# The second mixture of a fused attention kernel in blocks of 512 tokens in place of 256

## The chip, the cores and the metric

The kernel runs on one core of a Trainium2 chip. The metric is the time of one execution on the device in microseconds (us); the median of several executions stands for a kernel. A core has TensorE (PE; its weight loads stand in the profile as PEld), VectorE (DVE), ScalarE (ACT), GpSimd (POOL), and SyncE (SP), whose queue issues the transfers (DMA) here. TensorE writes its results to PSUM, in banks of 512 floats on each of 128 partitions; everything else lies in SBUF.

## What is computed

Causal attention with a bias from cumulated sums, then two dense mixtures one after the other, over 4 x 576 = 2304 tokens of 512 features, each with a hidden layer of 2048. All of it is in float32. The second mixture, which is the one changed, is the last function:

```python
# attention: batch, n_heads, seq, head_dim = (4, 8, 576, 64) -> x: 2304 x 512
def _moe_ref(x, w_in, w_out):              # first mixture
    h = x @ w_in                           # 2304 x 2048
    g = h * (1.0 / (1.0 + np.exp(-1.702 * h)))
    return g @ w_out                       # 2304 x 512

def _moe2_ref(x, w_in, w_out, s, b):       # second mixture
    h = x @ w_in
    r = np.maximum(h, 0.0)
    g = s * (r * r) + b
    return g @ w_out
```

## The kernel before

**Split operands.** A float32 operand of a matmul is split into two parts of the type fp32r: a copy rounded to that type, and the remainder (the value less its copy). A product takes three matmuls: weight remainder by token copy, copy by remainder, copy by copy. A split token or weight tile therefore has two halves, `[:, 0]` the copy and `[:, 1]` the remainder.

**Tiling.** The hidden layer is cut into 16 slices f of 128, the features into four chunks of 128. For a slice f, `h2` issues 4 x 3 = 12 matmuls with a 128 x 128 piece of the weights as the stationary operand and the tokens, as many as the block has, as the moving one. They add up in one PSUM bank `ph`. Then a chain of five instructions makes the gated values: Relu (ACT) into `r`, square and scale-and-shift (both DVE, in place), the rounded copy (ACT), the remainder (POOL for even f, DVE for odd f) into `g`. On the way out, for each 128 tokens t, three matmuls with a 128 x 128 piece of g as stationary operand and 512 columns of the output weights as the moving one add into a bank `py[t]`, over all f. When f = 15 is in, `py[t]` is copied to SBUF (ACT or DVE) and stored.

**Order.** TensorE's instructions stand in the order of the program text; a planner puts those of the other engines into each engine's queue, and they wait there for semaphores. `second` runs over a block of 256 tokens: hidden matmuls of f, then the out-matmuls of f - 4 (`LEAD = 4`). So from f = 4 to 15 twelve hidden matmuls of 256 columns alternate with six out-matmuls of 512 columns; at the end of a block five groups of out-matmuls (30) stand together, and behind them five groups of hidden matmuls (60) of the next block. There are nine blocks.

**Tokens and weights.** The first mixture leaves its result in DRAM (`x1_d`, feature by token). `load_x` brings a block of it back in one transfer of 512 KB and splits it with two ACT copies and two POOL subtractions of 512 columns each. The last unit of the first mixture, `first_whole`, frees the first mixture's weights slice by slice; `next_weights` then brings the second mixture's: 32 weights (w2i and w2o, 16 each) of 512 KB come as 8-byte words into 5 staging places (tag `pair`), and `load_w` turns each into floats and splits it with two ACT and three DVE instructions (L128 to L136). A staging place is free again when its weight is split. All of this is issued on SP's one queue.

**Buffers.** `ph` takes 3 banks, `py` 5. `g` has 10 places of 640 floats, one for the two halves of a slice; `r` has 2 places of 320 floats (tag `th`, which the first mixture uses as well). `xT` in the pool `xp` has 4 places of 640 floats, used by the first mixture's tokens.

Of the kernel before, what the change touches and what calls it, by code (L numbers as in the profile page):

```python
# [9 lines left out]
F32 = mybir.dt.float32  # L10
U32 = mybir.dt.uint32
F32R = mybir.dt.float32r
AF = mybir.ActivationFunctionType
ALU = mybir.AluOpType
# [3 lines left out]
P = 128  # L18
# [11 lines left out]
SPAN = 0.98  # L30
EARLY = 1.0
AHEAD, LEAD = 2, 4


def f32(ap):
    return ap.bitcast(F32)
# [27 lines left out]
def fused_kernel(ctx: ExitStack, tc: tile.TileContext, qkT, vP, s, w1i, w1o, w2i, w2o, s2, b2, out):  # L64
    nc = tc.nc
    B, H, _, _ = qkT.shape
    D, S = P // 2, s.shape[1]
    BH = B * H
    NT, C = out.shape
    NF, _, CM = w1i.shape  # L70
    NC = C // P
# [4 lines left out]

    first, second = [(0, 64), (64, 192), (192, 320)], [(320, 448), (448, 576)]
    units = [Unit(b, 0, first, []) for b in range(B)] + [Unit(b, 1, second, first) for b in range(B)]
    NMAX = max(u.n for u in units)

# [32 lines left out]
    def load_w(stage, src, tag, f):  # L113

        pool, stage_tag, bufs = stage
        if src.dtype == F32:
            single = pool.tile([P, 2 * CM], F32, tag=stage_tag, name="single", bufs=bufs)[:, :CM]
            nc.sync.dma_start(single, src[f])
        else:

            pair = pool.tile([P, 2 * CM], U32, tag=stage_tag, name="pair", bufs=bufs)
            nc.sync.dma_start(pair, src[f].bitcast(U32))
            lower, upper = pair[:, 0 : 2 * CM : 2], pair[:, 1 : 2 * CM : 2]
            nc.scalar.activation(f32(upper), f32(upper), AF.Prelu, scale=2.0**-112, alpha=2.0**32)  # L128
            nc.vector.tensor_scalar(out=lower, in0=lower, scalar1=2.0**-29, scalar2=7.49, op0=ALU.mult, op1=ALU.min)  # L129
            nc.vector.scalar_tensor_tensor(  # L130
                out=lower, in0=upper, scalar=3, in1=lower, op0=ALU.logical_shift_left, op1=ALU.bitwise_or
            )
            single = f32(lower)
        w = wp.tile([P, 2, CM], F32R, tag=tag, name=f"{tag}{f}")
        nc.scalar.activation(w[:, 0, :], single, AF.Copy)
        nc.vector.tensor_tensor(w[:, 1, :], single, f32(w[:, 0, :]), ALU.subtract)  # L136
        return w


    with ExitStack() as p1:  # L140
# [4 lines left out]
            out=mask[:, WIDE:], in_=mask[:, WIDE:], pattern=[[-1, P]], compare_op=ALU.is_ge,  # L145
# [330 lines left out]
                run(ui)  # L476


    N2 = 256
    rawp = ctx.enter_context(tc.tile_pool(name="rawp", bufs=5))  # L480
    psY = ctx.enter_context(tc.tile_pool(name="psY", bufs=5, space=PSUM))
    xp2 = ctx.enter_context(tc.tile_pool(name="xp2", bufs=2))
    wi2, wo2 = {}, {}

    def load_x(ti):
        raw = xp2.tile([P, NC, N2], F32, tag="xraw2", name="xraw2", bufs=1)
        nc.sync.dma_start(raw, x1_d[:, ti * N2 : (ti + 1) * N2].rearrange("(c p) t -> p c t", p=P))
        x = xp2.tile([P, 2, NC, N2], F32R, tag="xT2", name="xT2")
        for cc in range(0, NC, 2):
            nc.scalar.activation(x[:, 0, cc : cc + 2, :], raw[:, cc : cc + 2, :], AF.Copy)  # L490
            nc.gpsimd.tensor_tensor(x[:, 1, cc : cc + 2, :], raw[:, cc : cc + 2, :], f32(x[:, 0, cc : cc + 2, :]), ALU.subtract)
        return x

    def h2(f, x, g2):
        ph = psM.tile([P, 512], F32, tag="m", name="ph2")
        k = 0
        for cc in range(NC):
            wc = slice(cc * P, (cc + 1) * P)
            for a, b in ((1, 0), (0, 1), (0, 0)):
                nc.tensor.matmul(ph[:, :N2], wi2[f][:, a, wc], x[:, b, cc, :], start=(k == 0), stop=(k == 3 * NC - 1))  # L500
                k += 1
        r = gp.tile([P, NMAX], F32, tag="th", name="r", bufs=2)[:, :N2]
        nc.scalar.activation(r, ph[:, :N2], AF.Relu)  # L503
        nc.vector.tensor_tensor(r, r, r, ALU.mult)  # L504
        nc.vector.tensor_scalar(out=r, in0=r, scalar1=s_sb, scalar2=b_sb, op0=ALU.mult, op1=ALU.add)  # L505
        g = gp.tile([P, 2, NMAX], F32R, tag="g", name="g2")
        nc.scalar.activation(g[:, 0, :N2], r, AF.Copy)  # L507
        (nc.vector if f % 2 else nc.gpsimd).tensor_tensor(g[:, 1, :N2], r, f32(g[:, 0, :N2]), ALU.subtract)  # L508
        g2[f] = g

    def first_whole(ui):

        n, x = units[ui].n, split_x(ui)
        py = [psY.tile([P, 512], F32, tag="y", name="py3") for _ in range(NC)]
        for f in range(NF + LEAD):
            if f < NF:
                yield from h_item(ui, f, x)
                freed.append(("wi", f))
            if f >= LEAD:
                k = f - LEAD  # L520
                for c in range(NC):
                    for i, (a, b) in enumerate(((1, 0), (0, 1), (0, 0))):
                        nc.tensor.matmul(
                            py[c][:, :n], wo[k][:, a, c * P : (c + 1) * P], g_t[ui, k][:, b, :n],
                            start=(k == 0 and i == 0), stop=(k == NF - 1 and i == 2),
                        )
                freed.append(("wo", k))
                yield 12 * (n / 2.4 + 3)
        for c in range(NC):
            y = gp.tile([P, NMAX], F32, tag="y", name="y", bufs=4)  # L530
            if c % 2:
                nc.scalar.activation(y[:, :n], py[c][:, :n], AF.Copy, scale=0.5)
            else:
                nc.vector.tensor_scalar(out=y[:, :n], in0=py[c][:, :n], scalar1=0.5, scalar2=None, op0=ALU.mult)
            nc.sync.dma_start(x1_d[c * P : (c + 1) * P, t0_of[ui] : t0_of[ui] + n], y[:, :n])

    def second(ti, x):
        g2 = {}
        py = [psY.tile([P, C], F32, tag="y", name="py2") for _ in range(N2 // P)]
        for f in range(NF + LEAD):  # L540
            if f < NF:
                h2(f, x, g2)
                yield 12 * (N2 / 2.4 + 3)
            if f >= LEAD:
                k = f - LEAD
                for t in range(N2 // P):
                    for i, (a, b) in enumerate(((1, 0), (0, 1), (0, 0))):
                        nc.tensor.matmul(  # L548
                            py[t], g2[k][:, a, t * P : (t + 1) * P], wo2[k][:, b, :],
                            start=(k == 0 and i == 0), stop=(k == NF - 1 and i == 2),  # L550
                        )
                yield 6 * 216
        for t in range(N2 // P):
            y = xp2.tile([P, C], F32, tag="y2", name="y2", bufs=3)
            if t % 2:
                nc.scalar.activation(y, py[t], AF.Copy)
            else:
                nc.vector.tensor_copy(y, py[t])
            r0 = ti * N2 + t * P
            nc.sync.dma_start(out[r0 : r0 + P, :], y)  # L560

    freed = []
    with tc.manual_schedule(engines={PE}):
        def next_weights():
            for tag, f in freed:
                src, to = (w2i, wi2) if tag == "wi" else (w2o, wo2)
                to[f] = load_w((rawp, "pair", 5), src, tag, f)
            freed.clear()

        x2 = load_x(0)  # L570
        for _ in first_whole(len(units) - 1):
            next_weights()
        next_weights()
        for ti in range(NT // N2):
            x = x2
            for k, _ in enumerate(second(ti, x)):
                if k == NF // 2 and ti + 1 < NT // N2:
                    x2 = load_x(ti + 1)


# [41 lines left out]
```

## Time and profile before

| | us |
|---|---|
| Median of 3 executions (1089.58 to 1094.0) | 1090.66 |
| The profiled execution | 1089.36 |
| Its span, from the first to the last instruction | 1087.6 |
| TensorE busy in the span | 1031.3 |
| VectorE busy | 681.9 |
| ScalarE busy | 556.8 |
| GpSimd busy | 349.5 |
| Mean granted clock of TensorE, as a share of 2.4 GHz | 0.983 |

The profile shows one execution. Durations of TensorE's matmuls overlap, since they are pipelined and their ends are modelled; what one of them costs in a run is the distance from its start to the next one's start. A line such as L500 is a line of the kernel before. `A <- B` reads as output from inputs, by the program's names, and `x12` counts instructions. In a row of the order of time, the first number is the start and the second the time from the first start to the last end of the merged instructions; in brackets stands how long the engine was idle before and what it waited for.

### The profile page before, as it was taken

The page shows a single profiled execution, that of the slowest core. Times are in us where ns is not written, and L with a number is a line of the kernel's source. Part 1 is how long each engine was busy: PE and PEld are TensorE (multiplying, and loading weights), DVE is VectorE, ACT ScalarE, POOL GpSimd, SP SyncE. Part 2 cuts the span into 40 slices and gives each one's busy share as a digit, 9 for nine tenths or more (in the row PEclk, how much of TensorE's full clock was granted, in tenths as well). Part 3 has the DMA queues.
Part 4 walks back from the last instruction along what each step waited for, and adds up shares of the span by engine and source line. Part 5 has one row for each costly group of instructions (what it writes and reads, how often), then busy time and mean ns, then how long its engine had stood idle before and what let it go on. Part 6 is the DMA issues. An engine that isn't in the chain of part 4 may idle for free.

```text
span 1087.6 us, 19218 instructions
## 1 busy us (share of the span) xinstructions
PE 1031.3 (95%) x6984; PEld 952.9 (88%) x6984; DVE 681.9 (63%) x1600; ACT 556.8 (51%) x1378; POOL 349.5 (32%) x412
## 2 busy tenths in 40 slices
PE   4978999999989999999999998899999999999998
PEld 2447999999988999999999998799989999899997
DVE  4689777566467788877886598843434434344333
ACT  4788766556536646656666476532323323233232
POOL 1124445335344435544453341121221212112110
PEclk9968999999999999999999998899999999999999
DMA  6566332121042232223221478210110101100000
GB/s 197 155 240 202 101 88 68 54 87 43 10 130 70 69 99 73 84 73 90 74 85 37 168 227 245 78 40 1 40 36 4 40 1 39 39 1 20 2 20 20
DMA packets 40799, 85.64 MB, mean 79 GB/s; under 512 B 5344, under 2 KB 20064, under 8 KB 40704
## 3 DMA queue, kind: packets, MB, share of 16 engines
q1 hardware_dynamic: 40704, 84.41, 25.2%
q8 instruction: 55, 0.90, 0.4%
q14 instruction: 40, 0.33, 0.1%
HBM read 70.30 MB, written 10.03 MB: 74 GB/s over the span
## 4 chain that ended last, share of the span: by engine, by line
PE 73%; DVE 13%; DMA 7%; ACT 4%; issue 3%; SPq 1%; POOL 0%; DVEq 0%; ACTq 0%; POOLq 0%
PE py L548 18%; PE ph L500 18%; PE py L404 13%; PE ph L382 12%; PE ps L249 4%; PE pst L287 4%; PE po L314 3%; DVE hi L111 3%; DMA pair<-w1i 2%; DMA pair<-w2i 2%; DVE pair L130 2%; DMA pair<-w1o 1%; DVE pair L129 1%; DVE x L255 1%; ACT x L261 1%
## 5 line engine op out<-in xcount | busy, mean ns | idle before, releaser
L382 PE MATMUL ph<-xT,wi 128*128 128x320 f32 (+1 forms) x1536 | 246.7, 305 | 6.8 <-DVE th L388 4.2
L500 PEld LDWEIGHTS ph<-xT,wi 128*128 128x128 f32 x1728 | 222.9, 192 | 9.7 <-ACT r L503 0.8
L500 PE MATMUL ph<-xT,wi 128*128 128x256 f32 x1728 | 225.7, 284 | 0.6 <-ACT r L503 0.6
L382 PEld LDWEIGHTS ph<-xT,wi 128*128 128x128 f32 x1536 | 217.4, 193 | 9.3 <-DVE th L388 5.3
L548 PE MATMUL py<-wo,g 128*128 128x512 f32 x864 | 218.0, 395 | 3.2 <-POOL g L508 3.1
L404 PE MATMUL py<-g,wo 128*128 128x320 f32 (+1 forms) x1344 | 215.3, 304 | 1.4 <-DVE th L388 0.9
L404 PEld LDWEIGHTS py<-g,wo 128*128 128x128 f32 x1344 | 187.9, 189 | 2.5 <-DVE th L388 1.0
L548 PEld LDWEIGHTS py<-wo,g 128*128 128x128 f32 x864 | 156.4, 190 | 31.1 <-POOL g L508 3.4
L504 DVE TENSOR_TENSOR r<-r 128x256 f32<-128x256 f32 x144 | 61.7, 428 | 160.4 <-ACT r L503 159.3
L508 POOL TENSOR_TENSOR g<-r,g 128x256 fp32r<-128x256 f32 x72 | 54.4, 756 | 326.7 <-ACT g L507 283.4
L391 POOL TENSOR_TENSOR g<-th,g 128x320 fp32r<-128x320 f32 (+1 forms) x128 | 114.3, 894 | 113.2 <-ACT g L390 112.6
L261 ACT ACTIVATE x<-x,m 64x64 f32<-64x64 f32 (+2 forms) x160 | 89.5, 560 | 107.7 <-DVE m L255 105.8
L507 ACT ACTIVATE g<-r 128x256 fp32r<-128x256 f32 x144 | 60.1, 417 | 110.4 <-DVE r L505 110.4
L503 ACT ACTIVATE r<-ph 128x256 f32<-128x256 f32 x144 | 55.2, 383 | 117.1 <-PE ph L500 115.1
L229 POOL TENSOR_TENSOR lo<-raw,hi 64x576 fp32r<-64x576 f32 (+1 forms) x56 | 67.9, 1212 | 134.9 <-issue 63.4
L255 DVE CUSTOM_DVE_ANT_0 x<-ps,mask 64x64 f32<-64x64 f32 (+2 forms) x160 | 67.9, 426 | 58.5 <-PE ps L249 56.6
L287 PE MATMUL pst<-ident,x 128*128 128x128 f32 (+2 forms) x480 | 85.7, 286 | 11.1 <-DVE ph L296 9.0
L109 POOL TENSOR_SCALAR x<-x,tot 64x64 f32<-64x64 f32 (+1 forms) x96 | 48.6, 514 | 96.5 <-DVE tot L266 63.4
L293 ACT ACTIVATE ph<-pst 64x256 fp32r<-64x256 f32 (+2 forms) x144 | 67.0, 472 | 22.4 <-PE pst L287 20.7
L287 PEld LDWEIGHTS pst<-ident,x 128*128 128x128 f32 (+2 forms) x480 | 54.5, 135 | 25.8 <-DVE ph L296 13.9
L111 DVE TENSOR_SCALAR hi<-raw 128x832 fp32r<-128x832 f32 (+1 forms) x48 | 70.8, 1474 | 1.9 <-DMA vraw<-vP 1.7
L505 DVE TENSOR_SCALAR r<-r,s_sb,b_sb 128x256 f32<-128x256 f32 x144 | 67.4, 468 | 5.0
(69 smaller groups left out, 1331.3 us busy)
## 6 DMA issues: line engine op xcount, KB each, us to landing
raw<-qkT SPq DMA_DIRECT2D x32, 416.0 KB
pair<-w1o SPq DMA_DIRECT2D x16, 512.0 KB
pair<-w1i SPq DMA_DIRECT2D x16, 512.0 KB
pair<-w2i SPq DMA_DIRECT2D x16, 512.0 KB
pair<-w2o SPq DMA_DIRECT2D x16, 512.0 KB
raw<-qkT SPq DMA_DIRECT2D x24, 320.0 KB
vraw<-vP SPq DMA_DIRECT2D x16, 320.0 KB
xraw<-x_d SPq DMA_DIRECT2D x9, 512.0 KB
```

The source lines that it names most:

```text
L111: nc.vector.tensor_scalar(out=out, in0=in_, scalar1=scale, scalar2=None, op0=ALU.mult)
L229: nc.gpsimd.tensor_tensor(lo[:D, kc], raw[:D, kc], f32(hi[:D, kc]), ALU.subtract)
L255: nc.vector.tensor_tensor_reduce(out=x[:w, j0:j1], in0=ps[:w, : j1 - j0], in1=mask[:w, WIDE - a0 + j0 : WIDE - a0 + j1], scale=-1.0 / ROOT ...
L261: nc.scalar.activation(x[:w, :a1], x[:w, :a1], AF.Exp, bias=least, scale=-1.0, accum_out=tot[:w, c : c + 1])
L287: nc.tensor.transpose(ps[: j1 - j0, at : at + a1 - a0], t["x"][c][: a1 - a0, j0:j1], ident[: a1 - a0, : a1 - a0])
L293: nc.scalar.activation(t["ph"][:rows, base:end], ps[:rows, :m], AF.Copy)
L382: nc.tensor.matmul(ph[:, :n], w[:, a, wc], x[cc][:, b, :n], start=(k == 0), stop=(k == 3 * NC - 1))
L391: nc.gpsimd.tensor_tensor(g[:, 1, :n], th[:, :n], f32(g[:, 0, :n]), ALU.subtract)
L404: nc.tensor.matmul(py[:, :n], wo[f][:, a, wc], g_t[ui, f][:, b, :n], start=(k == 0), stop=(k == 3 * G - 1))
L500: nc.tensor.matmul(ph[:, :N2], wi2[f][:, a, wc], x[:, b, cc, :], start=(k == 0), stop=(k == 3 * NC - 1))
L505: nc.vector.tensor_scalar(out=r, in0=r, scalar1=s_sb, scalar2=b_sb, op0=ALU.mult, op1=ALU.add)
L548: nc.tensor.matmul(py[t], g2[k][:, a, t * P : (t + 1) * P], wo2[k][:, b, :], start=(k == 0 and i == 0), stop=(k == NF - 1 and i == 2),)
```

## The change

The second mixture runs over blocks of 512 tokens, four of them, and one of 256 for the last 256 tokens. The hidden matmuls are 512 columns wide in the wide blocks. The out-matmuls of a slice follow two slices behind its hidden matmuls in place of four. A block's tokens are loaded in four pieces of 128 features, through two raw buffers, and their split form stands in places of the weights' staging tag `pair`, which has nine places in place of five. The gated values of a slice take two tiles, so two of the ten places of `g`, in place of one. `r` takes places of the tag `xT`. The planner gets no cost hints from `second` any more; none were read there.

```diff
+WIDE2, LEAD2, PLACES = 512, 2, 9
...
-    N2 = 256
-    rawp = ctx.enter_context(tc.tile_pool(name="rawp", bufs=5))
+    rawp = ctx.enter_context(tc.tile_pool(name="rawp", bufs=PLACES))
...
-    def load_x(ti):
-        raw = xp2.tile([P, NC, N2], F32, tag="xraw2", name="xraw2", bufs=1)
-        nc.sync.dma_start(raw, x1_d[:, ti * N2 : (ti + 1) * N2].rearrange("(c p) t -> p c t", p=P))
-        x = xp2.tile([P, 2, NC, N2], F32R, tag="xT2", name="xT2")
-        for cc in range(0, NC, 2):
-            nc.scalar.activation(x[:, 0, cc : cc + 2, :], raw[:, cc : cc + 2, :], AF.Copy)
-            nc.gpsimd.tensor_tensor(x[:, 1, cc : cc + 2, :], raw[:, cc : cc + 2, :], f32(x[:, 0, cc : cc + 2, :]), ALU.subtract)
-        return x
+    blocks = [(t, min(WIDE2, NT - t)) for t in range(0, NT, WIDE2)]
+
+    def load_x(t0, n):
+        parts = []
+        for cc in range(NC):
+            raw = xp2.tile([P, WIDE2], F32, tag="xraw2", name="xraw2")
+            nc.sync.dma_start(raw[:, :n], x1_d[cc * P : (cc + 1) * P, t0 : t0 + n])
+            x = rawp.tile([P, 2, WIDE2], F32R, tag="pair", name="xT2")
+            nc.scalar.activation(x[:, 0, :n], raw[:, :n], AF.Copy)
+            nc.gpsimd.tensor_tensor(x[:, 1, :n], raw[:, :n], f32(x[:, 0, :n]), ALU.subtract)
+            parts.append(x)
+        return parts
...
-                nc.tensor.matmul(ph[:, :N2], wi2[f][:, a, wc], x[:, b, cc, :], start=(k == 0), stop=(k == 3 * NC - 1))
+                nc.tensor.matmul(ph[:, :n], wi2[f][:, a, wc], x[cc][:, b, :n], start=(k == 0), stop=(k == 3 * NC - 1))
...
-        r = gp.tile([P, NMAX], F32, tag="th", name="r", bufs=2)[:, :N2]
-        nc.scalar.activation(r, ph[:, :N2], AF.Relu)
+        r = xp.tile([P, 2 * NMAX], F32, tag="xT", name="r")[:, :n]
+        nc.scalar.activation(r, ph[:, :n], AF.Relu)
...
-        g = gp.tile([P, 2, NMAX], F32R, tag="g", name="g2")
-        nc.scalar.activation(g[:, 0, :N2], r, AF.Copy)
-        (nc.vector if f % 2 else nc.gpsimd).tensor_tensor(g[:, 1, :N2], r, f32(g[:, 0, :N2]), ALU.subtract)
+        g = [gp.tile([P, 2 * NMAX], F32R, tag="g", name="g2")[:, :n] for _ in range(2)]
+        nc.scalar.activation(g[0], r, AF.Copy)
+        (nc.vector if f % 2 else nc.gpsimd).tensor_tensor(g[1], r, f32(g[0]), ALU.subtract)
...
-    def second(ti, x):
+    def second(t0, n, x):
         g2 = {}
-        py = [psY.tile([P, C], F32, tag="y", name="py2") for _ in range(N2 // P)]
-        for f in range(NF + LEAD):
+        py = [psY.tile([P, C], F32, tag="y", name="py2") for _ in range(n // P)]
+        for f in range(NF + LEAD2):
             if f < NF:
-                h2(f, x, g2)
-                yield 12 * (N2 / 2.4 + 3)
-            if f >= LEAD:
-                k = f - LEAD
-                for t in range(N2 // P):
+                h2(f, x, n, g2)
+                yield f
+            if f >= LEAD2:
+                k = f - LEAD2
+                for t in range(n // P):
...
-                to[f] = load_w((rawp, "pair", 5), src, tag, f)
+                to[f] = load_w((rawp, "pair", PLACES), src, tag, f)
...
-        for ti in range(NT // N2):
+        for k, (t0, n) in enumerate(blocks):
             x = x2
-            for k, _ in enumerate(second(ti, x)):
-                if k == NF // 2 and ti + 1 < NT // N2:
-                    x2 = load_x(ti + 1)
+            for f in second(t0, n, x):
+                if f == NF // 2 and k + 1 < len(blocks):
+                    x2 = load_x(*blocks[k + 1])
```

## Rows read from the trace of the kernel before

**Rows 1.** The page, busy time and share of the span of each engine.
```profile
PE 1031.3 (95%) x6984; PEld 952.9 (88%) x6984; DVE 681.9 (63%) x1600; ACT 556.8 (51%) x1378; POOL 349.5 (32%) x412
```

**Rows 2.** Stretches: length, busy us of PE, PEld, DVE, ACT, POOL, clock, DMA share, GB/s.
```profile
640.00:660.00 20.00, 20.00 (x169) 20.00 (x168) 19.64 (x36) 15.27 (x32) 6.50 (x7) 1.00 0.81 239
660.00:671.00 11.00, 7.76 (x41) 7.07 (x41) 9.73 (x17) 6.55 (x14) 3.19 (x3) 0.70 0.72 210
671.00:683.00 12.00, 8.23 (x63) 7.82 (x63) 9.20 (x20) 7.35 (x17) 0.76 (x1) 0.93 0.82 256
683.00:697.00 14.00, 13.97 (x73) 12.38 (x73) 13.51 (x28) 8.83 (x20) 2.28 (x2) 0.81 0.37 110
```

**Rows 3.** TensorE's waits from 660 us on: total us, times, longest us.
```profile
PE py L548 <- POOL g L508: 3.1, 1, 3.1
...
```

**Rows 4.** TensorE in order of time, the start of block 0.
```profile
671.16 5.95 PE L500 MATMUL ph<-xT,wi 128*128 128x256 f32 x48
...
682.57 2.93 PE L548 MATMUL py<-wo,g 128*128 128x512 f32 x6 [3.15 <-POOL g L508]
```

**Rows 5.** The chain that ended last, in order of time: start, us, what.
```profile
716.71 6.83 PE py L548 x30
...
761.75 6.83 PE py L548 x30
```

**Rows 6.** TensorE in order of time, from 718.0 us: inside a run.
```profile
717.71 5.83 PE L548 MATMUL py<-wo,g 128*128 128x512 f32 x25
```

**Rows 7.** TensorE in order of time, from block 0 to block 1.
```profile
713.73 1.55 PE L548 MATMUL py<-wo,g 128*128 128x512 f32 x6
715.12 1.60 PE L500 MATMUL ph<-xT,wi 128*128 128x256 f32 x12
716.55 6.99 PE L548 MATMUL py<-wo,g 128*128 128x512 f32 x30
723.38 7.36 PE L500 MATMUL ph<-xT,wi 128*128 128x256 f32 x60
730.57 1.55 PE L548 MATMUL py<-wo,g 128*128 128x512 f32 x6
```

**Rows 8.** All engines in order of time, the last gating chains of the last block.
```profile
1076.18 0.74 POOL L508 TENSOR_TENSOR g<-r,g 128x256 fp32r<-128x256 f32 x1 [4.90 <-issue]
...
1077.13 0.39 ACT L503 ACTIVATE r<-ph 128x256 f32<-128x256 f32 x1 [1.08 <-PE ph L500]
1077.55 0.43 DVE L504 TENSOR_TENSOR r<-r 128x256 f32<-128x256 f32 x1 [1.95 <-ACT r L503]
1078.01 0.42 DVE L505 TENSOR_SCALAR r<-r,s_sb,b_sb 128x256 f32<-128x256 f32 x1
1078.46 0.42 ACT L507 ACTIVATE g<-r 128x256 fp32r<-128x256 f32 x1 [0.94 <-DVE r L505]
1078.91 0.43 DVE L508 TENSOR_TENSOR g<-r,g 128x256 fp32r<-128x256 f32 x1 [0.48 <-ACT g L507]
```

**Rows 9.** Groups from 690 us on: busy us, mean ns of one, idle before.
```profile
L491 POOL TENSOR_TENSOR xT<-xraw,xT 128x512 fp32r<-128x512 f32 x14 | 19.0, 1378 | 8.3 <-ACT xT L490 8.3
...
L556 ACT ACTIVATE y<-py 128x512 f32<-128x512 f32 x9 | 5.4, 597 | 40.7 <-PE py L548 40.7
```

**Rows 10.** The staging tile, 605 to 700 us: ns minimum, median, maximum.
```profile
L136 DVE TENSOR_TENSOR wo<-pair,wo x16: 675/680/1227, 636.5 to 695.8; 128x512 fp32r<-128x512 f32 x16
```

**Rows 11.** All engines in order of time, two token conversions on POOL beside DVE.
```profile
717.69 1.54 DVE L505 TENSOR_SCALAR r<-r,s_sb,b_sb 128x256 f32<-128x256 f32 x1
...
719.71 0.95 DVE L508 TENSOR_TENSOR g<-r,g 128x256 fp32r<-128x256 f32 x1 [0.48 <-ACT g L507]
```

**Rows 12.** SP's queue in order of time: block 1's tokens, the sixth weight.
```profile
620.40 0.38 SPq L487 DMA_DIRECT2D xraw<-x_d  x1
622.40 0.33 SPq L126 DMA_DIRECT2D pair<-w2o  x1
```

**Rows 13.** The chain that ended last: one of the last weights on its way.
```profile
674.05 6.50 DMA pair<-w2i
```

More of the change, by code (lines that the diff above doesn't have):

```diff
@@ L483, in fused_kernel, with h2 @@
     wi2, wo2 = {}, {}
-    def load_x(ti):
-        raw = xp2.tile([P, NC, N2], F32, tag="xraw2", name="xraw2", bufs=1)
-        nc.sync.dma_start(raw, x1_d[:, ti * N2 : (ti + 1) * N2].rearrange("(c p) t -> p c t", p=P))
-        x = xp2.tile([P, 2, NC, N2], F32R, tag="xT2", name="xT2")
-        for cc in range(0, NC, 2):
-            nc.scalar.activation(x[:, 0, cc : cc + 2, :], raw[:, cc : cc + 2, :], AF.Copy)
-            nc.gpsimd.tensor_tensor(x[:, 1, cc : cc + 2, :], raw[:, cc : cc + 2, :], f32(x[:, 0, cc : cc + 2, :]), ALU.subtract)
-        return x
-    def h2(f, x, g2):
+    blocks = [(t, min(WIDE2, NT - t)) for t in range(0, NT, WIDE2)]
[9 more added lines that the diff above has]
+        return parts
+    def h2(f, x, n, g2):
         ph = psM.tile([P, 512], F32, tag="m", name="ph2")
@@ L535, in first_whole @@
             nc.sync.dma_start(x1_d[c * P : (c + 1) * P, t0_of[ui] : t0_of[ui] + n], y[:, :n])
-    def second(ti, x):
+    def second(t0, n, x):
         g2 = {}
-        py = [psY.tile([P, C], F32, tag="y", name="py2") for _ in range(N2 // P)]
-        for f in range(NF + LEAD):
+        py = [psY.tile([P, C], F32, tag="y", name="py2") for _ in range(n // P)]
+        for f in range(NF + LEAD2):
             if f < NF:
-                h2(f, x, g2)
-                yield 12 * (N2 / 2.4 + 3)
-            if f >= LEAD:
-                k = f - LEAD
-                for t in range(N2 // P):
+                h2(f, x, n, g2)
[3 more added lines that the diff above has]
+                for t in range(n // P):
                     for i, (a, b) in enumerate(((1, 0), (0, 1), (0, 0))):
                         nc.tensor.matmul(
-                            py[t], g2[k][:, a, t * P : (t + 1) * P], wo2[k][:, b, :],
+                            py[t], g2[k][a][:, t * P : (t + 1) * P], wo2[k][:, b, :],
                             start=(k == 0 and i == 0), stop=(k == NF - 1 and i == 2),
                         )
-                yield 6 * 216
-        for t in range(N2 // P):
+        for t in range(n // P):
             y = xp2.tile([P, C], F32, tag="y2", name="y2", bufs=3)
@@ L558, in second @@
                 nc.vector.tensor_copy(y, py[t])
-            r0 = ti * N2 + t * P
-            nc.sync.dma_start(out[r0 : r0 + P, :], y)
+            nc.sync.dma_start(out[t0 + t * P : t0 + (t + 1) * P, :], y)
     freed = []
@@ L566, in next_weights @@
                 src, to = (w2i, wi2) if tag == "wi" else (w2o, wo2)
-                to[f] = load_w((rawp, "pair", 5), src, tag, f)
+                to[f] = load_w((rawp, "pair", PLACES), src, tag, f)
             freed.clear()
-        x2 = load_x(0)
+        x2 = load_x(*blocks[0])
         for _ in first_whole(len(units) - 1):
```

## The prediction

> **What bounds the kernel now.** I read the page's engine shares first: TensorE is busy for 95% of the span [rows 1]. Its matmul ends are modelled, so that number only says where to look. Next come the busy times by stretch. From 640 to 697 us something else rules: in the last 20 us of the first mixture DVE has no room left (19.64 of 20), and in the three stretches behind it TensorE stands still for 7 us and the granted clock sinks to 0.70, 0.93 and 0.81 of 2.4 GHz, that is, it falls to 1.2 GHz for part of each [rows 2]. The waits of TensorE from 660 us on name what ended last there: the longest, 3.1 us, is for gated values g of the second mixture from POOL [rows 3], and it ends at 682.57 us, when that mixture has run for 11 us [rows 4]. Behind that TensorE waits for nobody: the chain of waits from 697 us to the end is TensorE's two kinds of matmul and nothing else, and it repeats with a period of 761.75 - 716.71 = 45.04 us per block of 256 tokens [rows 5]. So two stages matter here: nine blocks that TensorE's own matmul rate bounds, and the handover from first to second mixture, bound by DVE and by the weights' arrival.
>
> **What a matmul costs.** A change of width is priced by distances of starts, not by mean durations, which overlap. In an unbroken run, 25 matmuls of 512 columns start between 717.71 us [rows 6] and 723.38 us, and 60 of 256 columns between 723.38 and 730.57 us [rows 7]: 226.8 and 119.8 ns. Against 213.3 and 106.7 ns of pure columns at 2.4 GHz each carries about 13 ns that doesn't depend on its width. Where both widths alternate, six wide ones take 715.12 - 713.73 = 1.39 us, 231.7 ns each, and twelve narrow ones 1.43 us, 119.2 ns [rows 7]. So the change of width itself costs 6 x 4.9 - 12 x 0.6 = 22 ns a round.
>
> **The change part by part.**
> *Width.* Tokens 0 to 2047 go from eight blocks of 256 to four of 512; the last 256 tokens stay a block of 256. A wide block has 192 matmuls into the hidden layer (twelve for each of 16 slices f) and 192 out of it (2 x 96), all 512 columns wide. At 226.8 ns that is 384 x 226.8 = 87.09 us in place of 2 x 45.04 = 90.08: 2.99 us a block, 12.0 us in four. Most of it is 768 fixed parts that go, the rest the change of width. Bounds: if every wide matmul costs 231.7 ns, as in the alternation, a block takes 88.97 us and four save 4.4 us; more than 12.0 needs a rate that no row shows. I take 12.0: an unbroken run of one width is what the new block is.
> The Trainium skill ("TensorE: Matmul & The Clock Gate", section "Back-to-back issue gap") gives the isolated distance as columns / 2.4 GHz plus 2.5 ns, which speaks against this change. By it four wide blocks would save only 768 x 2.5 = 1.9 us; the trace disagrees with 13 ns, and the sum goes by the trace.
>
> *Lead 2 in place of 4.* The hidden slice f is used two slices later, so the gating chain (Relu, square, scale and shift, copy, remainder) must end within four twelve-matmul runs, 10.9 us, and at a block's start and end, where runs of one kind stand together, within two: 5.44 us less about 0.16 us of the last matmul's drain, 5.28. At 256 columns the chain's five pieces add up to 2.09 us and its handovers to 0.2 [rows 8]. At 512 I take 0.60 each for Relu and copy (the eviction of the same size), 0.68 each for square, scale and a DVE remainder (the weights' subtraction of that size) and 1.38 for a POOL remainder [rows 9, 10]: 3.4 us for odd f, 4.2 for even f. Both fit, so the loss is nothing while nothing stands in the queues. That cover can go: while POOL converts tokens, a scale and shift took 1.54 us in place of 0.41 and a remainder 0.95 in place of 0.43 [rows 8, 11]. The tokens of the block after next find free places when a block's last hidden slice is done, so up to three conversions of 1.38 us fall on the chain of f = 15, at the ends of three blocks. It grows by 1.7 us x 3/2 = 2.5 and waits for up to two copies, 1.2 us more: 7.1 us against 5.28, at most 1.8 us three times, 5.5 in all; at least nothing. I take 0.4 in all, since before only two pieces of such a chain were stretched. The last, narrow block has two narrow runs, 24 x 119.8 less the drain = 2.7 us, for a chain of 0.39 + 0.43 + 0.42 + 0.42 + 0.74 (POOL) + 0.3 = 2.7: I take 0.3, bounds 0 and 0.7.
>
> *Tokens in the weights' places.* Staging grows from 5 places to 9, the block's four token tiles take 4, so 5 are left to the weights, as before. Token bytes and conversions are the same; each load comes as four of 256 KB on SP's queue in place of one of 512 KB. Two raw buffers make the third and fourth load wait for POOL's conversions, with weight loads queued behind on SP; before, SP already stood that way until 620.40 us for the next tokens [rows 12]. The first weights are under way by then and DVE works them off, so I price it at nothing; uncovered, it is some 3 us later weights.
>
> *Gated values in two tiles, r in xT's places.* Ten places hold five slices; with lead 2, four at most are alive. r gets four buffers for two. Nothing, while the places last.
>
> *The handover.* Undisturbed, the stretch from the first hidden matmul of a block to its last is 45.04 - 6.83 = 38.2 us; in block 0 it takes 716.71 - 671.16 = 45.5 [rows 4, 5], so 7.3 us are lost, to the wait for g at 682.57 us and to the low clock behind it. After: three wide runs (8.2 us) can go ahead of the first use, where five narrow ones (7.2 us) can now; but the first g needs wider pieces in a DVE queue full of weights, and the next block's tokens come onto POOL as places come free. I take a loss of 0.5 us. Bounds: a gain of 3 (the low clock's share falls away) and a loss of 6 (one wait and one half-rate stretch more).
>
> *Sum:* -12.0 + 0.4 + 0.3 + 0.5 = -10.8 us. The profiled execution took 1089.36 us (span 1087.6), so 1078.6 us; the median stands 1.3 above it: **1079.9 us**.
>
> **The rivals.**
> *The alternation's price stays* (10%): 231.7 ns for wide matmuls, if the extra comes from the change of output rather than of width. -4.4 + 1.2 = -3.2: 1087.5 us. For it: the extra stands at the first matmuls of a run. Against: both kinds of neighbour differ in width.
> *Waits eat the gain* (13%): block ends and handover near their upper bounds, +6 us in place of +1.2: about 1085 us, reaching 1089. For it: DVE's full stretch; against: 5.3 us of cover for 3.4 to 4.2.
> *Hardly any fixed cost* (4%): the wide hidden matmuls take nearly twice a narrow one, with 2.5 ns saved a pair: 768 x 2.5 = 1.9 us less 1.2, 1090 us. Only a sight of a hidden matmul 512 wide refutes it; both unbroken runs speak against it. The skill's sentence above is this rule.
> *The tokens starve the weights, slower* (7%): SP's queue before shows token loads ahead of weights that stand earlier in the program [rows 12], so block 1's four tiles could take places 5 to 8 while weights still come, and leave one. A weight then costs its transfer (6.5 us where the chain followed one [rows 13]) and its five pieces on ACT and DVE (at most 5 x 0.68 = 3.4 us [rows 10]) in a row, some 9.9 us, where the stream now brings one in 0.524 MB / 239 GB/s = 2.2 us [rows 2]. TensorE waits from about the third such weight on, since block 0 uses two in 5.4 us. From 671 us on 256 GB/s x 12 us and 110 x 14 still come [rows 2], 4.6 MB or some nine weights: 9 x 7.7 = 69 us, of which the 42 us more that a wide block 0 lasts cover a part: +27 on the forecast's -11, 1107 us.
> *More is gained at the handover* (4%): 1075 us.
> The forecast itself has 62%, with 1076 to 1084 us as its own range.
>
> **The numbers.** A median of three here tells about 0.5%, 5.5 us, from nothing. Faster by more: the forecast, the last rival and a third of the second, 0.70. Within: the first, the third and most of the second, 0.22. Slower: 0.08. The range, 1075 to 1089, takes in both bounds of the width and most of the waits.
>
> **What would show it.** Right: twelve hidden matmuls start over 2.72 us; blocks 1 to 3 repeat with 87.1 us, the narrow block has 45; TensorE waits for nothing from some 700 us on; block 0's first out-matmul waits to about 684 us; the last weight lands near 690 us. Wrong: rounds of 5.56 us instead of 5.44 (alternation), waits for g at block ends (lead), weight loads some 8 us apart (places), or a low clock behind 700 us.

## The result and the profile after

The changed kernel takes 1075.76 us (median of four executions, 1074.44 to 1076.01) against 1090.12 us before (four, 1088.86 to 1094.0). The ratio is 0.9866, 95% interval 0.9843 to 0.989: 14.6 us faster, between 12.0 and 17.1 (the two medians lie 14.4 apart). The forecast was 10.8 us faster, a little less than that interval allows; the time lies in the range, near its lower end.

The page of the changed kernel, engine shares, to be held against [rows 1]: TensorE has 768 matmuls fewer and 10.7 us less busy time.

```profile
PE 1020.6 (95%) x6216; PEld 912.4 (85%) x6216; DVE 641.1 (60%) x1440; ACT 536.2 (50%) x1252; POOL 347.2 (32%) x382
```

The chain that ended last in the changed kernel, in order of time (start, us, what), the answer to [rows 5]. L554 is the out-matmul (L548 before), L506 the hidden one (L500).

```profile
754.39 8.28 PE py L554 x36
762.67 8.16 PE ph L506 x36
...
841.55 8.31 PE py L554 x36
849.86 8.16 PE ph L506 x36
...
928.74 8.16 PE py L554 x36
936.90 8.16 PE ph L506 x36
...
1015.78 8.16 PE py L554 x36
```

The reader is to see two things. Both kinds of matmul now take 8.16 / 36 = 0.2267 us, and the wide blocks repeat with 87.16, 87.19 and 87.04 us, where 87.09 was foretold and two narrow blocks took 90.08. Second, two of the closing runs are 0.12 and 0.15 us longer than 8.16: that is all that the short lead costs at the ends of wide blocks.

TensorE in order of time through the handover, the answer to [rows 4, 7]: start, time, instructions, and in brackets the idle time and what ended it.

```profile
661.69 0.58 PE L529 MATMUL py<-g,wo 128*128 128x256 f32 x1 [2.41 <-ACT g L393]
662.55 5.22 PE L529 MATMUL py<-g,wo 128*128 128x256 f32 x23 [0.27 <-POOL g L394]
667.61 8.33 PE L506 MATMUL ph<-xT,wi 128*128 128x512 f32 x36
680.51 4.61 PE L554 MATMUL py<-wo,g 128*128 128x512 f32 x12 [4.58 <-POOL g L514]
684.95 2.92 PE L506 MATMUL ph<-xT,wi 128*128 128x512 f32 x12
687.71 2.88 PE L554 MATMUL py<-wo,g 128*128 128x512 f32 x12
690.43 2.88 PE L506 MATMUL ph<-xT,wi 128*128 128x512 f32 x12
...
701.31 2.88 PE L506 MATMUL ph<-xT,wi 128*128 128x512 f32 x12
705.13 3.02 PE L554 MATMUL py<-wo,g 128*128 128x512 f32 x12 [0.94 <-POOL g L514]
```

Twelve matmuls of either kind start over 2.72 us (690.43 - 687.71). The first out-matmul of block 0 waits to 680.51 us, twelve of them then take 4.44 us from start to start in place of 2.72, with a granted clock of 0.62 from 680.5 to 685 us, that is 1.2 GHz for most of it, and one more wait of 0.94 us follows. L529 is the out-matmul of the first mixture's last unit. TensorE's waits from 660 us on, against [rows 3]:

```profile
PE py L554 <- POOL g L514: 5.8, 3, 4.6
PE py L529 <- ACT g L393: 2.4, 1, 2.4
PE py L529 <- POOL g L394: 0.3, 1, 0.3
```

The third of the three waits for g is in the narrow block at 1028.52 us (0.27 us idle; with its late start the first out-matmul comes 0.43 us behind its place).

**Where the 13.5 us of the two profiled executions went** (span 1087.6 to 1074.1). I cut the span at two places: the start of the first mixture's last unit, `first_whole`, and the start of the run of out-matmuls that closes block 0.

| Stretch, us | before | after |
|---|---|---|
| Up to first_whole | 615.70 | 614.66 |
| Handover: first_whole and block 0 up to its closing run | 100.85 | 139.57 |
| the same without any wait, at full clock | 84.3 | 124.9 |
| so lost in the handover | 16.5 | 14.6 |
| Closing run of block 0 to the end of the span | 371.05 | 319.87 |

The line without waits is worked out: first_whole has 384 matmuls at 119.8 ns, 46.0 us; block 0 up to its closing run has 192 hidden matmuls, and with lead 4 eleven rounds of out-matmuls, with lead 2 thirteen: 192 x 119.8 ns + 66 x 231.7 ns = 38.3 us before, 348 x 226.8 ns = 78.9 us after. In the handover block 0 covers twice the tokens, so stretches two and four are to be read together: 84.3 + 371.05 = 455.3 us before, 124.9 + 319.87 = 444.8 after, 10.6 less. That is the 12.0 us of the width, less the waits that the short lead brought (0.3 at two block ends, 0.4 in the narrow block) and less a tail that is 0.8 us longer: from TensorE's last matmul to the end of the span it takes 4.5 us in place of 3.7. That isn't chance, since the second profile of the changed kernel has 4.5 too, and so have lead 3 alone and lead 4 alone below; all other profiles have 3.7. Why is not known. The handover loses 1.9 us less than before, and 1.0 us lies ahead of first_whole, where the text of the program is the same but for the loads of block 0's tokens.

### The profile page after: what moved, and what is told of

The parts are those of the page before. It is cut to its first block, busy times and chain, and to the rows that moved or that the text cites. A ratio compares the mean times of both kernels' runs of the same rounds, so it can differ in the third digit from the quotient of the medians.

```text
span 1074.1 us, 17311 instructions
## 1 busy us (share of the span) xinstructions
PE 1020.6 (95%) x6216; PEld 912.4 (85%) x6216; DVE 641.1 (60%) x1440; ACT 536.2 (50%) x1252; POOL 347.2 (32%) x382
## 4 chain that ended last, share of the span: by engine, by line
PE 72%; DVE 12%; ACT 5%; DMA 5%; issue 4%; POOL 1%; SPq 1%; DVEq 0%; ACTq 0%; POOLq 0%
PE py L554 17%; PE ph L506 17%; PE py L407 13%; PE ph L385 12%; PE ps L252 5%; PE pst L290 4%; PE po L317 3%; DVE hi L114 3%; DVE pair L133 1%; DMA pair<-w1i 1%; DVE x L258 1%; ACT x L264 1%; DVE pair L132 1%; DMA pair<-w2i 1%; DMA xraw<-x_d 1%
## 5 line engine op out<-in xcount | busy, mean ns | idle before, releaser
L385 PEld LDWEIGHTS ph<-xT,wi 128*128 128x128 f32 x1536 | 216.5, 193 | 8.6 <-ACT xT L368 3.8
L554 PE MATMUL py<-wo,g 128*128 128x512 f32 x864 | 209.8, 392 | 5.8 <-POOL g L514 5.8
L506 PE MATMUL ph<-xT,wi 128*128 128x512 f32 (+1 forms) x960 | 208.4, 368 | 0.0
L554 PEld LDWEIGHTS py<-wo,g 128*128 128x128 f32 x864 | 162.2, 189 | 40.4 <-POOL g L514 6.8
L506 PEld LDWEIGHTS ph<-xT,wi 128*128 128x128 f32 x960 | 169.1, 188 | 31.0
L510 DVE TENSOR_TENSOR r<-r 128x512 f32<-128x512 f32 (+1 forms) x80 | 54.2, 678 | 209.4 <-ACT r L509 209.4
L514 POOL TENSOR_TENSOR g<-r,g 128x512 fp32r<-128x512 f32 (+1 forms) x40 | 50.1, 1252 | 314.9 <-PE py L554 170.0
L509 ACT ACTIVATE r<-ph 128x512 f32<-128x512 f32 (+1 forms) x80 | 44.3, 553 | 151.3 <-PE ph L506 151.1
L513 ACT ACTIVATE g<-r 128x512 fp32r<-128x512 f32 (+1 forms) x80 | 47.0, 587 | 91.9 <-DVE r L511 91.9
L290 PEld LDWEIGHTS pst<-ident,x 128*128 128x128 f32 (+2 forms) x480 | 54.9, 136 | 24.2 <-DVE ph L299 13.4
L391 DVE SCALAR_TENSOR_TENSOR th<-th,ph 128x320 f32<-128x320 f32 (+1 forms) x128 | 57.4, 448 | 23.0 <-ACT th L390 21.9
```

Of the source, the lines that this page charges most:

```text
L290: nc.tensor.transpose(ps[: j1 - j0, at : at + a1 - a0], t["x"][c][: a1 - a0, j0:j1], ident[: a1 - a0, : a1 - a0])
L385: nc.tensor.matmul(ph[:, :n], w[:, a, wc], x[cc][:, b, :n], start=(k == 0), stop=(k == 3 * NC - 1))
L391: nc.vector.scalar_tensor_tensor(out=th[:, :n], in0=th[:, :n], scalar=1.0, in1=ph[:, :n], op0=ALU.add, op1=ALU.mult)
L506: nc.tensor.matmul(ph[:, :n], wi2[f][:, a, wc], x[cc][:, b, :n], start=(k == 0), stop=(k == 3 * NC - 1))
L554: nc.tensor.matmul(py[t], g2[k][a][:, t * P : (t + 1) * P], wo2[k][:, b, :], start=(k == 0 and i == 0), stop=(k == NF - 1 and i == 2),)
```

## The experiments

Each ratio is to the kernel before, timed beside it on the same chip, with its 95% interval. Each run left a profile, and the table gives the loss in its handover, worked out as above (with lead 3 and 4 block 0 has twelve and eleven rounds of out-matmuls ahead of its closing run, so 336 and 324 wide matmuls), and what follows up to the end of the span.

| Kernel | ratio | handover lost, us | rest, us |
|---|---|---|---|
| before, first and second profile | 0.9995 (0.9976 to 1.0013) | 16.5, 15.1 | 371.0, 371.0 |
| before with lead 2 | 1.0105 (1.008 to 1.0129) | 18.3 | 375.5 |
| changed, blocks of 256, lead 4 | 0.999 (0.9973 to 1.0007) | 13.0 | 371.0 |
| changed, first and second profile | 0.9866 (0.9843 to 0.989), 0.9877 (0.9849 to 0.9905) | 14.6, 13.7 | 319.9, 319.8 |
| changed, 2 places for weights | 0.9868 (0.9828 to 0.9907) | 10.5 | 320.2 |
| changed, weights first | 0.9853 (0.9828 to 0.9878) | 10.9 | 319.1 |
| changed, lead 3 | 0.9839 (0.9816 to 0.9863) | 9.7 | 321.8 |
| lead 3, 3 places for weights | 0.9811 (0.9795 to 0.9828) | 8.9 | 320.9 |
| lead 3, weights first | 0.9807 (0.9778 to 0.9836) | 7.9 | 320.9 |
| lead 3, 3 places, weights first | 0.979 (0.9768 to 0.9811) | 7.0 | 320.9 |
| changed, lead 4 | 0.9791 (0.9761 to 0.9821) | 5.1 | 324.4 |
| lead 4, weights first | 0.976 (0.9744 to 0.9775) | 3.9 | 323.7 |

(The rest grows by 2.7 us for each further slice of lead, since the closing run is longer by twelve matmuls; the handover is shorter by as much. The 0.8 us between kernels of one lead in the last column are the longer tail named above; only the 320.2 holds something else, late waits of block 0.)

**The width alone.** Blocks of 256 and lead 4, all other edits left in:

```diff
-WIDE2, LEAD2, PLACES = 512, 2, 9
+WIDE2, LEAD2, PLACES = 256, 4, 9
```

> The changed kernel with its blocks put back to 256 tokens and the lead to 4; token loads in pieces, their places among the weights' and the two g tiles stay. Theory A (the terms: 12 us come from the width alone, and the 2.5 us that the end of the first mixture gained come from token loads standing ahead of the weights on SP): blocks repeat with 45.0 us, the stretch of first_whole lasts about 53 us as in the changed kernel, and the time is the before kernel's less 2.5 us, about 1087.6. Rival B (the 2.5 us are chance between executions, or need the wide block): first_whole lasts 55.5 us again and the time is the before kernel's within 1 us. Rival C (the places or the two g tiles gave the gain and the width little): about 1078.

Ratio 0.999, 1.1 us faster than before, between 2.9 faster and 0.8 slower. Its chain repeats with 45.04 us as before:

```profile
758.48 6.83 PE py L554 x30
765.31 7.19 PE ph L506 x60
...
803.52 6.83 PE py L554 x30
810.35 7.19 PE ph L506 x60
```

So rival C falls: without the width nearly all of the gain is gone. Between A and B the time doesn't decide; the profile is A's for the handover (first_whole took 50.6 us, loss 13.0), but A's reason for it is tested below. The other edits, which stay in here, are together worth nothing that this ratio tells from noise.

**The lead alone.** Lead 2 in the kernel before, in blocks of 256:

```diff
-        for f in range(NF + LEAD):
+        for f in range(NF + 2):
...
-            if f >= LEAD:
-                k = f - LEAD
+            if f >= 2:
+                k = f - 2
```

> The before kernel with nothing changed but the lead of the out-matmuls in the second mixture, 2 in place of 4. Theory A: a narrow block has two narrow runs, 2.7 us, for a chain of 2.7 to 3.0 us at its start, so TensorE waits some 0.3 to 0.6 us for g of f = 0 in each of nine blocks, and where POOL converts tokens beside the chain of f = 15 more: in all 3 to 8 us slower, 1093 to 1098. Rival: the planner's queue orders hide the shorter lead, within 1 us of before.

Ratio 1.0105, 11.4 us slower, more than expected. TensorE in order of time, one block and the next:

```profile
722.16 4.69 PE L548 MATMUL py<-wo,g 128*128 128x512 f32 x18
726.70 4.46 PE L500 MATMUL ph<-xT,wi 128*128 128x256 f32 x36
731.37 1.67 PE L548 MATMUL py<-wo,g 128*128 128x512 f32 x6 [0.21 <-POOL g L508]
...
768.16 4.70 PE L548 MATMUL py<-wo,g 128*128 128x512 f32 x18
```

The period is 46.0 us in place of 45.04 from block 1 to block 7, and 45.55 in block 8, where POOL has no more tokens to convert at the end of the block before. Eighteen closing out-matmuls take 4.54 us where 18 x 0.2268 and the change of width make 4.11; 36 hidden ones and the wait behind them 4.67 us where 36 x 0.1198 makes 4.31. So the chain misses its cover at both ends of a narrow block, some 7.2 us in all, and the handover loses more (18.3 us). In a wide block the same lead in slices is twice as long in time, and next to nothing was lost at the block ends. What it costs in the first block is measured with leads 3 and 4 below.

**Block 0's tokens behind the first weights.** The order of loads on SP's queue, which theory A held for the cause of the better handover:

```diff
-        x2 = load_x(*blocks[0])
+        x2, n_w = None, 0
         for _ in first_whole(len(units) - 1):
+            n_w += len(freed)
             next_weights()
+            if x2 is None and n_w >= 5:
+                x2 = load_x(*blocks[0])
```

> The changed kernel with block 0's token loads put behind the first weights in the program, so that SP's queue holds six weight loads ahead of the tokens and all nine places take weights at first. Theory A: the weights' split falls on DVE ahead of the gating of first_whole again, TensorE waits at the start of first_whole as before the change, and that stretch lasts 55 us or more in place of 53: 2 to 4 us slower than the changed kernel, 1078 to 1080. Rival B (the order of the loads has no part in it): within 1 us of the changed kernel's 1075.8. Rival D (more weights in flight early relieve the handover): faster than 1074.

Ratio 0.9853: not slower, and within the interval of the changed kernel's 0.9866, so between B and D the time doesn't decide. The wait for DVE at the start of first_whole did come back (0.6 us), but first_whole took 48.2 us, less than in any kernel so far, and the handover lost 10.9 us, though the weights are split earlier (from 614.1 us on; 617.9 before, 623.2 in the changed kernel). Theory A's order of loads isn't what makes the handover better as a whole.

**The same kernels again**, each with a second profile.

> The changed kernel once more, with another profile. Theory E (the stretch of first_whole is chance: its waits hang on how ACT, DVE, POOL and the transfers meet in one execution, so it varies by some us between executions of one kernel, while the second mixture doesn't): the second mixture, from its first hidden to its last out matmul, takes 401.6 us within 1, and first_whole anything from 48 to 55. Rival A (first_whole's 52.9 us belong to the changed kernel): 52.9 within 0.7 again.

> The before kernel once more, with another profile. Theory E: the second mixture takes 412.3 us within 1 and first_whole anything from 48 to 56. Rival A: first_whole takes 55.5 us within 0.7 again.

The changed kernel: 0.9877; first_whole 49.8 us (52.9 the first time), second mixture up to its last out-matmul 403.8 us (401.6). Before: 0.9995 against itself; first_whole 56.0 (55.5), second mixture 410.4 (412.3). Theory E was right that first_whole varies from one execution to the next, by 3 us in the changed kernel (before, it repeated within 0.5 us, as rival A had it), and wrong that the second mixture doesn't: what first_whole loses less, block 0 loses more. Taken together the two repeat within 1.4 us: 16.5 and 15.1 us lost before, 14.6 and 13.7 after. So the handover comes out better by about 1.7 us, hardly more than the scatter, which two profiles each don't make sure of, and only the sum of the two stretches can be read.

One part of it repeats. TensorE at the start of first_whole, first in the kernel before, then in the changed one:

```profile
615.70 4.48 PE L382 MATMUL ph<-xT,wi 128*128 128x256 f32 x36
621.31 1.70 PE L382 MATMUL ph<-xT,wi 128*128 128x256 f32 x12 [1.12 <-DVE th L388]
623.37 1.69 PE L382 MATMUL ph<-xT,wi 128*128 128x256 f32 x12 [0.36 <-DVE th L388]
```

```profile
614.66 7.36 PE L385 MATMUL ph<-xT,wi 128*128 128x256 f32 x60
621.86 1.60 PE L529 MATMUL py<-g,wo 128*128 128x256 f32 x12
```

And why, by DVE in order of time before (the first weight's split stands ahead of the first gating, L388) and after (L391 is the gating, L132 the first weight):

```profile
618.03 1.20 DVE L129 TENSOR_SCALAR pair<-pair 128x512 uint32<-128x512 uint32 x1 [1.70 <-DMA pair<-w2i]
619.34 1.59 DVE L130 SCALAR_TENSOR_TENSOR pair<-pair 128x512 uint32<-128x512 uint32 x1
620.85 0.41 DVE L388 SCALAR_TENSOR_TENSOR th<-th,ph 128x256 f32<-128x256 f32 x1
```

```profile
616.78 0.42 DVE L391 SCALAR_TENSOR_TENSOR th<-th,ph 128x256 f32<-128x256 f32 x1 [1.49 <-ACT th L390]
618.22 0.42 DVE L391 SCALAR_TENSOR_TENSOR th<-th,ph 128x256 f32<-128x256 f32 x1 [1.02 <-ACT th L390]
...
623.68 0.54 DVE L132 TENSOR_SCALAR pair<-pair 128x512 uint32<-128x512 uint32 x1
```

The four token loads let the first weight's transfer start only at 618.19 us, where it started at 613.02 before, and the first gating no longer stands behind it. Up to 640 us TensorE waits there for DVE 1.6 to 1.8 us in the three profiles with the old loads (before, its repeat, lead 2 in narrow blocks), for nobody in the seven with the new ones, and 0.6 us in the four with the weights first. That this order shortens the handover as a whole isn't shown: the kernels with the weights first lose less in it than their twins (10.9 against 14.6 and 13.7, 7.9 against 9.7, 7.0 against 8.9, 3.9 against 5.1 us), and why stays open.

**Staging places.** The prediction's slower rival, weights short of places, made real:

```diff
-WIDE2, LEAD2, PLACES = 512, 2, 9
+WIDE2, LEAD2, PLACES = 512, 2, 6
```

> The changed kernel with 6 staging places in place of 9: block 0's tokens take four, two are left to the weights. This prices the prediction's rival that tokens starve the weights, without its full severity. Theory A (a weight holds its place for its transfer and five pieces, some 8 to 10 us, so two places give one weight in 4 to 5 us in place of 2.2): the split of the last weight ends some 60 us later, near 750 us; DVE is free for first_whole, which then lasts 46 to 49 us and no longer 50 to 55; block 0 uses two weights in 5.4 us and gets them every 8 to 10, so it lasts 30 to 60 us longer: 1100 to 1130. Rival (weights were limited by DVE and not by places, so two places nearly do): within 5 us of the changed kernel.

Ratio 0.9868: the rival to that expectation is right, two places do as well as five. The staging tile's last split (DVE, ns minimum, median, maximum, first and last start), and the stretches (length, busy us of PE, PEld, DVE, ACT, POOL, clock, DMA share, GB/s):

```profile
L139 DVE TENSOR_TENSOR wo<-pair,wo x16: 677/692/1032, 644.9 to 740.4; 128x512 fp32r<-128x512 f32 x16
```

```profile
620.00:640.00 20.00, 20.00 (x169) 20.00 (x168) 10.77 (x21) 11.17 (x26) 8.61 (x10) 1.00 0.63 185
640.00:660.00 20.00, 19.99 (x168) 19.78 (x166) 12.93 (x25) 11.87 (x26) 6.19 (x7) 1.00 0.49 154
```

The second stretch in the changed kernel, and in the one with lead 4 and the weights first:

```profile
640.00:660.00 20.00, 18.55 (x151) 17.94 (x149) 18.80 (x35) 13.54 (x28) 4.35 (x5) 1.00 0.79 241
640.00:660.00 20.00, 20.00 (x169) 20.00 (x168) 19.69 (x35) 15.46 (x32) 6.32 (x6) 1.00 0.75 240
```

The last weight is split 43 us later than in the changed kernel (740.4 against 697.5 us), and it doesn't matter: block 0 lasts long enough for it. DVE has room in first_whole (12.93 of 20 us busy, 18.80 in the changed kernel), and TensorE works through; but a full DVE alone doesn't hold it up, since with lead 4 it works through beside 19.69 us of DVE. What comes back is 2.3 us of lost time near the end of block 0, 1.3 of it in the closing run and so in the table's last column. The weights weren't short of places here. That they came too early isn't shown: the time is the same as with five places, and the kernel that splits them earlier, with the weights first, loses no more (10.9 and 10.5 us).

**A longer lead in the wide blocks**, alone and with the weights first:

```diff
-WIDE2, LEAD2, PLACES = 512, 2, 9
+WIDE2, LEAD2, PLACES = 512, 3, 9
```

> The changed kernel with a lead of 3 in place of 2 (four slices of g alive, eight of the ten places). Theory A: the 4.6 us wait for the first g of block 0 shrinks by one hidden run of 2.7 us, and the waits at block ends and in the narrow block (0.3 and 0.5 us) go: 3 to 4 us faster than the changed kernel, about 1072. Rival: the first g is late because DVE and ACT are full of weights and later g's are late in turn, so the wait only moves to the second or third g: within 1 us of 1075.8.

> The changed kernel with a lead of 3 and block 0's token loads behind the first weights, both edits together. Theory F (lead 3 takes the waits of block 0 and of the block ends, the earlier weights take waits from first_whole; the two act in different stretches and add up): second mixture 399.5 us, first_whole 48 to 50, and 4 to 5 us faster than the changed kernel. Rival E (first_whole is chance, so only the lead counts): as lead 3 alone, 3 us faster.

Lead 3 alone: 0.9839, by the ratios about 3 us faster than the changed kernel, as expected, though the intervals overlap; the handover loses 9.7 us against 14.6 and 13.7, which is more than the scatter. The waits at block ends and in the narrow block are gone, and the wait for block 0's first g fell from 4.6 us (5.9 in the repeat) to 3.6, by 1.0 to 2.3 us where 2.7 was expected: the rival may be right in part. With the weights first as well: 0.9807, some 6 us faster than the changed kernel where theory F had 4 to 5, and a loss of 7.9 us against 9.7. The two gains come together, as theory F said; whether they add up in full the scatter doesn't tell.

**Lead 3 with seven places, three for weights**, in either order of loads:

```diff
-WIDE2, LEAD2, PLACES = 512, 2, 9
+WIDE2, LEAD2, PLACES = 512, 3, 7
```

> The changed kernel with lead 3 and 7 staging places, so three are left to the weights beside block 0's tokens. Theory G (the handover is bound by DVE and ACT: weights that come at the pace at which the wide block 0 uses them, two in 5.4 us, take DVE from nobody): the handover, from first_whole to block 0's last hidden matmul, loses 7 to 9 us to waits and low clock where lead 3 with five weight places lost 9.4, and the kernel takes 0.979 to 0.983 of before. Rival (fewer places only move the waits into block 0, as with two places): 0.984 or more.

> The changed kernel with lead 3, 7 staging places and block 0's token loads behind the first weights. Theory G and the order together: not slower than lead 3 with that order and nine places, 0.978 to 0.982 of before. Rival (the two take the same waits away, or with seven places taken by weights first the tokens come late): 0.983 or more.

0.9811 and 0.979, each inside theory G's bounds; but against nine places (0.9839 and 0.9807) the intervals overlap, and the losses differ by 0.8 and 0.9 us, no more than two profiles of one kernel. Fewer places do no harm; that they help isn't settled.

**Lead 4**, with the weights first and alone:

```diff
-WIDE2, LEAD2, PLACES = 512, 2, 9
+WIDE2, LEAD2, PLACES = 512, 4, 9
```

> The changed kernel with a lead of 4 and block 0's token loads behind the first weights. Five slices of g take all ten places. Theory: block 0's wait for its first g (3.3 us with lead 3) shrinks again by a hidden run of 2.7 us at most, but a slice's g has to wait for a place until the slice five before has been used, so the gain is a part of that: 0 to 2 us faster than lead 3 with the same order. Rival (g's places become the bound in every round): waits for POOL's g in all blocks, 3 us or more slower than lead 3.

> The changed kernel with a lead of 4 and nothing else. Theory (lead and order of the loads take different waits and add up): with lead 3 the weights-first order took the handover's loss from 9.7 to 7.9 us, with lead 4 that order left 3.9, so lead 4 alone should lose about 5.7, and the kernel take 0.978 of before. Rival (lead 4 does all, the order nothing): loss 4 to 4.5 us, 0.976.

With the weights first: 0.976, 1061.92 us (1061.72 to 1063.96), 26 us faster than before and the fastest kernel here, some 5 us faster than lead 3 where 0 to 2 were expected. TensorE's handover:

```profile
664.06 13.79 PE L506 MATMUL ph<-xT,wi 128*128 128x512 f32 x60
678.53 3.06 PE L554 MATMUL py<-wo,g 128*128 128x512 f32 x12 [0.68 <-POOL g L514]
681.42 2.88 PE L506 MATMUL ph<-xT,wi 128*128 128x512 f32 x12
```

Five hidden runs (13.6 us) now cover the first gating chain but for 0.68 us, and the low clock that followed the long wait is gone: the out-matmuls behind the wait take 2.89 us, not 4.44. That is why more was gained than the wait alone: 3.18 us of wait with lead 3 became 0.68, and the loss fell by 4.0. The feared wait for g's ten places didn't come: TensorE waits for nothing from 680 us on. Lead 4 alone takes 0.9791 and loses 5.1 us, between the two expectations (5.7 and 4 to 4.5), which the scatter doesn't tell apart. Its only edit to the changed kernel is the lead, so lead 2 in place of 4 costs the kernel some 8 us by the ratios (0.9866 and 0.9791), and it stands in the handover (14.6 and 13.7 us lost against 5.1).

## Why the prediction was right, and where it was short

**The price of a matmul: right.** Both kinds at 512 columns take 226.7 ns, as read from the unbroken run before, not the 231.7 ns of the alternation. The first rival (1087.5 us) and the third (1090 us, hardly any fixed cost) fall with it; the second (waits eat the gain, 1085 us) falls by the time itself. The Trainium skill's 2.5 ns for an isolated matmul ("TensorE: Matmul & The Clock Gate", section "Back-to-back issue gap") is too small for these rows: four wide blocks came out nearly 3 us shorter each, some 0.5 of it the change of width that is gone, where 2.5 ns left half a microsecond.

**The lead: right in sum.** Foretold were 0.4 us at block ends and 0.3 in the narrow block; it was 0.3 and 0.4. The mechanism at a block's end is the one described. After block 0's last hidden slice, all engines of the changed kernel in order of time:

```profile
754.49 0.60 ACT L509 ACTIVATE r<-ph 128x512 f32<-128x512 f32 x1 [0.79 <-PE ph L506]
755.12 1.07 DVE L510 TENSOR_TENSOR r<-r 128x512 f32<-128x512 f32 x1 [4.16 <-ACT r L509]
756.22 0.55 DVE L511 TENSOR_SCALAR r<-r,s_sb,b_sb 128x512 f32<-128x512 f32 x1
757.05 0.63 ACT L495 ACTIVATE xT<-xraw 128x512 fp32r<-128x512 f32 x1 [1.97 <-DMA xraw<-x_d]
757.59 0.62 ACT L513 ACTIVATE g<-r 128x512 fp32r<-128x512 f32 x1
757.76 2.99 POOL L496 TENSOR_TENSOR xT<-xraw,xT 128x512 fp32r<-128x512 f32 x2 [2.13 <-ACT xT L495]
758.24 1.36 DVE L514 TENSOR_TENSOR g<-r,g 128x512 fp32r<-128x512 f32 x1 [1.47 <-ACT g L513]
```

Relu starts at 754.49 and the remainder is done at 759.60 us, 5.1 us against a cover of 5.28; the closing run still grew by 0.12 us, so it fits with nothing to spare. The square (0.69 without POOL's reads beside it) and the remainder are stretched, and the copy starts 0.8 us late, behind a token copy that had itself waited for its transfer. The Trainium skill's page "SBUF — State Buffer" (section "Who interferes with whom") says that a DVE instruction with two SBUF inputs contends with a GpSimd instruction that reads SBUF; these rows agree, 1.36 us beside the token conversion in place of 0.69.

**Tokens in the weights' places: mis-sized.** The prediction priced it at nothing, or, uncovered, at "some 3 us later weights", and took later weights for a loss. They came 5 us later, and one thing was better for it: waits of 1.7 us at the start of first_whole went, because DVE (19.80 of 20 us busy from 620 to 640 us before, 16.78 after) met the first gating before the first weight. Whether the handover as a whole gained by it isn't shown, as said above. The slower rival, tokens that starve the weights, rested on weights being wanted as early as they came. With two places in place of five nothing was lost. Its price of 1107 us was for one place, which no run has, and its condition didn't arise: in the changed kernel block 1's tokens take their first places at 690.7 us, when the last weight's transfer has been issued (686.7 us).

**The handover: half a microsecond of loss foretold, 1.7 us of gain found** (two profiles each, 1.4 us of scatter, so even the sign isn't sure). Block 0's first out-matmul waited to 680.51 us, not to 684, and TensorE waited once more at 705.13 us, where it was to wait for nothing from 700 us on. The wide blocks with their lead may well cost something there: against the kernel with narrow blocks and the new places the loss is 14.6 and 13.7 in place of 13.0 us, the sign and about the size foretold, though within the scatter. What the prediction lacked is a price for what the other edits do to this stretch: with them and nothing else the loss is 13.0 us in one profile, 16.5 and 15.1 before. And it weighed three wide runs ahead of the first use only against five narrow ones. Five wide ones, lead 4, would have left a loss of 5.1 us: most of the gain that could be had here, some 9 us, the change gave away with its shorter lead.

Together, for the two profiled executions: -12.0 for the width, +0.7 for the lead, +0.8 for the longer tail, -1.9 in the handover and -1.0 ahead of first_whole make -13.4 of the measured -13.5, where -12.0 + 0.7 + 0.5 was foretold. The terms of the width and of the lead were right. That the kernel was faster still rests on a handover term hardly beyond the scatter and on 1 us in a stretch that the change hardly touches: in these profiles first_whole starts anywhere between 613.4 and 617.4 us. So the cause of the surplus stays open.

## What to carry to other kernels

Price a change of shape by distances of starts in unbroken runs of one shape, and look at alternating runs by themselves: the means in the profile hide both the fixed part and the cost of changing. A lead counts in time, not in slices: two slices that fell short at the ends of narrow blocks nearly sufficed at the ends of wide ones. But don't halve it because the blocks double. Look for the one place where it is used cold, the first block, which repaid each further slice of lead with 3 to 5 us here. Where the engine that prepares data is full, look at whose work stands first in its queue; here the first weight's split ahead of the first gating cost TensorE 1.7 us of waits.

## What the runs showed that I had not expected

The low clock behind a wait can cost nearly as much as the wait. In the changed kernel a wait of 2.41 us at the end of first_whole is followed by 23 matmuls of 256 columns that take 5.06 us from start to start in place of 2.8, at a granted clock of 0.54 from 662 to 668 us; the 4.58 us wait for block 0's first g is followed by twelve that take 1.7 us more than they need. With lead 4 and the weights first the waits there are under 0.8 us, and the granted clock from 660 to 683 us (changed kernel first, same columns as above) is 1.00 in place of 0.81:

```profile
660.00:683.00 23.00, 16.46 (x67) 13.93 (x68) 20.85 (x38) 16.56 (x31) 3.84 (x3) 0.81 0.75 248
660.00:683.00 23.00, 20.86 (x98) 16.97 (x97) 20.99 (x40) 16.90 (x31) 3.62 (x2) 1.00 0.77 255
```

And DVE's pieces of one chain don't grow alike from 256 to 512 columns: the scale and shift, which reads one tensor, from 0.41 to 0.55 us in the median, the square, which reads two, from 0.42 to 0.69. The prediction had 0.68 for both.
